# A linear-attention scan feeding a soft mixture of experts: forward scans moved to the head of a slot, the chunk states copied, and the output mixed between the down products

## The chip, the cores and the metric

One core of a Trainium2 chip runs the whole kernel in one launch. Its engines are called as the profile calls them: PE (TensorE, with PEld for its weight loads), DVE (VectorE), ACT (ScalarE), POOL (GpSimd) and SP (SyncE, which here only issues DMAs). The metric is the device time of one execution in microseconds (us), the median of several runs. All data is fp32.

## The reference, cut to what matters

```python
B, H, S, D = 4, 8, 768, 48                  # r, k, v, w: B x H x S x D;  u: H x D
for t in range(S):                          # linear attention with a decaying state
    cur = outer(u * k[t], v[t])
    y[t] = r[t] @ (state + cur)             # state: B x H x 48 x 48
    state = w[t][:, None] * state + outer(k[t], v[t])
x = y as (3072 tokens, 384)
logits = x @ phi                            # 32 slots = 8 experts x 4
d = softmax of logits over the tokens;  slot_input = d.T @ x
for e in range(8):                          # F = 1024
    slot_out[e] = relu(slot_input[e] @ w1[e]) @ w2[e]
out = softmax of logits over the slots @ slot_out
```

## The kernel before, in words

**Chunks.** The 768 steps of a head are cut into 6 chunks of 128. Inside a chunk the recurrence becomes matrix products: with G the product of decays from a step to the end of its chunk and its reciprocal counterpart from the start, keys are multiplied by G and queries by the forward products. Scores of a chunk are keys against queries, masked to earlier steps, and what comes from earlier chunks goes through a state of 48 x 48 at each chunk border. The term with u (the bonus) is a number a for each step and head, multiplied into v; the product is the tile `av`.

**Slots.** Two heads are worked on together, so there are 16 slots j = 4b + g (batch b, pair of heads g). The 128 partitions hold heads 2g and 2g+1 at partitions 0 to 47 and 64 to 111, and the 16 partitions left over by each carry a third of heads 6 and 7. So three units n0 = 3b, n0+1, n0+2 carry a batch, and in the fourth slot (g = 3) the keys and queries are put together in `g4` by six small DMAs from SBUF to SBUF (`gather`, two for each unit).

A slot does, on PE: `e_kn` (transpose the scaled keys, L565), `e_scores` (L575, 24 matmul records), `e_u` (L611, what each chunk adds to the state), `e_av` (L633, masked scores of the slot before against v), `e_a` (L591, the bonus numbers), `e_inter` (L640 adds `av` of the even head with an identity as weights, L647 adds queries times state). On DVE: three masked evictions of scores (L584), `state` (L620, a scan along the chunks that writes `Se`), `f_scan` (L525, L526, forward products of one unit), `g_scan` (L518, backward products), half of `c_y` (L657, y plus `av` into x). On POOL: a mask on a fourth of the scores (L581, after an ACT copy, L580), `p_k` (L535) and `p_r` (L539), which multiply keys and queries in place by the products, `p_rk` (L531), `p_av` (L606). On ACT: evictions. The scan `Se` is kept as [48, 6], chunk innermost, and is the moving operand of L647 with a step of 6 numbers; there is one `Se`.

In three of four slots a unit is prepared for the next slot (`state_n`: `f_scan`, then `p_r`) and another for the slot after it (`state_g`: `g_scan`, then `p_k`). Three of four slots also hold a piece of the expert part for the batch before: `x_turn` (L92, L660), `l_mm` (L97), `s_max`, `s_exp`, `s_mm` (L136), `s_norm`. A dummy matmul (`fill`, L489) stands at the end of each slot.

**What sets the order.** The schedule is written out by hand: each engine runs its instructions in the order of the program text, in one queue, and semaphores make it wait for its operands. The loop is in L730 to L808. In it `state(j)` stands after `e_inter(j - 1)`, `f_scan` after `state`, `p_r` after `f_scan`. All DMAs go through SP's queue in program order: keys and queries (`ld_kr`), decays (`ld_w`), values (`ld_v`), gathers, and the expert weights in pieces of 512 KB (`ld_w1`, `ld_w2`). PSUM has four rotating banks (`rot`) and four fixed ones (`cst`, `up`, `y0`, `y1`). SBUF is cut into 16 bins; expert weights are loaded into bins whose first contents are no longer needed.

**After the loop** (L813 to L901): the last slot's y, the logits of the last batch, the slot softmax brought together (`m_spread`, `m_factor`, `m_den`, `m_slots`), `up_proj` (L218), `turn`, then for a column group of 256 and one of 128 (`COLS`): `down_proj` (L251), `so_rep` (L258 to L261), `mix` (L276 to L283: products into four banks, evictions by DVE and ACT, a DMA to the output). `range_check` between the groups sets a flag; if a product of decays left its range, a slower form of the whole is run.

Of the kernel before, what the change touches and what calls it, by code (L numbers as in the profile page):

```python
# [18 lines left out]
P = 128  # L19
# [24 lines left out]
N_FILL0 = 14  # L44
N_FILL = (1,) * NIT
N_CHAIN = 2
W1_BINS = (9, 10, 11, 12, 13, 14, 15, 3)
W2_BINS = (4, 5, 6, 7, 8, 0, 2, 1)
PIECES = (0, 1, 1, 1, 1, 1, 1, 2, 1, 2, 1, 2, 2, 2, 1, 1)
SHARED = (0, 1, 1, 1) + (1,) * 12  # L50
PE_HEADS = (0,)
COLS = ((0, 256), (256, 384))
# [3 lines left out]
def rwkv_soft_moe(ctx: ExitStack, tc: tile.TileContext, wl, krl, vl, um, phil, w1l, w2l, r, k, v, w, u, out):  # L56
# [12 lines left out]
    nc.vector.tensor_reduce(out=r32.rearrange("p o s -> p (o s)"),  # L69
                            in_=ident.rearrange("p (g s) -> p s g", s=NS), axis=AX.X, op=ALU.add)  # L70
    rmat = const.tile([P, 4, NS], F32, name="rmat")
    nc.vector.tensor_copy(out=rmat, in_=r32.broadcast_to([P, 4, NS]))
    other = const.tile([TG, NTG, NS], F32, name="other")
    nc.vector.tensor_scalar(other, r32[0:TG].broadcast_to([TG, NTG, NS]), -BIG, BIG, op0=ALU.mult, op1=ALU.add)
# [4 lines left out]
    asum = const.tile([P, 2, C], F32, name="asum")  # L79
    cn = const.tile([P, NT, NS], F32, name="cn")  # L80
# [102 lines left out]
    def m_factor(b, q, bc):  # L183
        new = nM[:, b % 2:b % 2 + 1]
        bm = small.tile([TG, NTG, NS], F32, name="bm", bufs=1)
        nc.vector.tensor_tensor(out=bm, in0=bc, in1=other, op=ALU.add)
        mt = small.tile([TG, 1], F32, name="mt")
        nc.vector.tensor_reduce(out=mt, in_=bm, axis=AX.XY, op=ALU.min)
        fr = small.tile([TG, 1], F32, name="fr")
        nc.scalar.activation(out=fr, in_=new, func=AF.Exp, bias=mt, scale=-1.0)  # L190
        q["rf"] = rf = small.tile([TG, NS], F32, name="rf")
        nc.vector.tensor_scalar(rf, r32[0:TG, 0], fr, None, op0=ALU.mult)

    def m_den(q, bank):
        dp = bank([P, 1, NS], "den")
        nc.tensor.matmul(out=dp[:, 0, :], lhsT=ssum.broadcast_to([TG, P]), rhs=q["rf"], start=True, stop=True)
        q["den"] = den = small.tile([P, 1, NS], F32, name="den")
        nc.vector.tensor_scalar(den, dp, 1e-9, None, op0=ALU.add)
        nc.vector.reciprocal(out=den, in_=den)

    def m_slots(q, siT, bank):
# [3 lines left out]
        for st_ in range(2):  # L205
# [3 lines left out]
            nc.vector.tensor_tensor(  # L209
                out=dst, in0=sT.rearrange("p k (g a j) -> p k g a j", g=4, a=2)[:, :, :, st_],  # L210
                in1=q["den"].broadcast_to([P, KT, NS]).rearrange("p k (g a j) -> p k g a j", g=4, a=2)[:, :, :, st_],
                op=ALU.mult)
# [32 lines left out]
    def down_proj(hT, so, w2t, cg):  # L245
        lo, hi = COLS[cg]
        for st_ in range(2):
            for ft in range(FT):
                for g in range(4):
                    e = 4 * st_ + g  # L250
                    nc.tensor.matmul(  # L251
                        out=so[32 * g:32 * g + NS, :], lhsT=hT[ft // 2].rearrange(
                            "p (f e s) -> p f e s", f=2, e=E)[:, ft % 2, e, :],
                        rhs=w2t[e][:, FT * lo + ft * (hi - lo):FT * lo + (ft + 1) * (hi - lo)],
                        start=(st_ == 0 and ft == 0), stop=(st_ == 1 and ft == FT - 1))

    def so_rep(so, so_sb, rep, bank):
        nc.vector.tensor_copy(out=so_sb, in_=so)  # L258
        rp = bank(list(so_sb.shape), "rp")
# [11 lines left out]
    def mix(cT, rep, o, row, bank, parts=((0, 4), (4, 6))):  # L271
        ov = o.rearrange("p (n q t) -> p q n t", q=4, t=P)
        for lo, hi in parts:
            ops = [bank([P, hi - lo, P], "op") for _ in range(4)]
            for q in range(4):
                nc.tensor.matmul(out=ops[q].rearrange("p n t -> p (n t)"), lhsT=rep[32 * q:32 * q + NS, :],  # L276
                                 rhs=cT[32 * q:32 * q + NS, lo * P:hi * P], start=True, stop=True)
            for q in range(4):
                if q % 2:
                    nc.scalar.copy(out=ov[:, q, lo:hi, :], in_=ops[q])  # L280
                else:
                    nc.vector.tensor_copy(out=ov[:, q, lo:hi, :], in_=ops[q])
            nc.sync.dma_start(out=out[row:row + P, 512 * lo:512 * hi], in_=o[:, 512 * lo:512 * hi])  # L283
# [3 lines left out]
    def recompute():  # L287
# [114 lines left out]
        with tc.tile_pool(name="f_w", bufs=E) as f_w, tc.tile_pool(name="f_t", bufs=1) as f_t, \  # L402
# [32 lines left out]
            for cg, (lo, hi) in enumerate(COLS):  # L435
                so = f_pa.tile([P, hi - lo], F32, name="so")
                down_proj(hT, so, ws[1], cg)
                so_rep(so, so_sb[:, lo:hi], rep[:, lo:hi], bank)
                for row in range(lo, hi, P):
                    mix(cT, rep[:, row:row + P], o, row, bank)  # L440
# [25 lines left out]
    pat = cut(2, X + C * D, C * D)  # L466
    kr_b = [cut(3 + n, 0, KRW) for n in range(4)]
    w_b = [cut(3 + n, KRW, WC) for n in range(2)]
    G_b = [cut(6 + n, KRW, WC) for n in range(2)]
    v_b = [cut(n, KRW + lo, 2 * C * D) for n, lo in ((3, WC), (4, WC), (5, 576), (6, WC))]  # L470
    av = cut(5, KRW, 2 * C * D).rearrange("p (h c e) -> p h c e", h=2, e=D)
    g4 = cut(7, 0, KRW)
    kn = cut(7, KRW + WC, (C - 1) * PITCH).rearrange("p (c e) -> p c e", e=PITCH)
    at_b = [[[cut(8, 384 * (4 * n + 2 * h + hf), 384).rearrange("p (c t) -> p c t", t=P) for hf in range(2)]
             for h in range(2)] for n in range(2)]
    raw = cut(14, 0, 2 * S)
# [16 lines left out]
    def ld_w(n, lo=0, hi=C):  # L493
        a, z = CP * lo, CP * hi + 1
        nc.sync.dma_start(out=w_b[n % 2][:, a:z], in_=wl[n][:, a:z])

    def ld_kr(n, lo=0, hi=C):
        nc.sync.dma_start(out=kr_b[n % 4][:, 0:2 * S].rearrange("p (a t) -> p a t", a=2)[:, :, lo * P:hi * P],
                          in_=krl[n][:, :, lo * P:hi * P])

# [14 lines left out]
    def g_scan(n, lo=0, hi=C):  # L515
        G, wt = G_b[n % 2], w_b[n % 2]
        a, z = CP * lo, CP * hi + 1
# [11 lines left out]
    def p_rk(n, src=None):  # L529
        kr = kr_b[n % 4] if src is None else src  # L530
        nc.gpsimd.tensor_tensor(out=rk_b[n % 2], in0=kr[:, 0:S], in1=kr[:, S:2 * S], op=ALU.mult)  # L531

    def p_k(n, lo=0, hi=C):
        kv = kr_b[n % 4][:, lo * P:hi * P].rearrange("p (c t) -> p c t", t=P)
        nc.gpsimd.tensor_tensor(out=kv, in0=kv, in1=chunks(G_b[n % 2], 2, lo, hi), op=ALU.mult)  # L535

    def p_r(n, lo=0, hi=C):
        rv = kr_b[n % 4][:, S + lo * P:S + hi * P].rearrange("p (c t) -> p c t", t=P)
        nc.gpsimd.tensor_tensor(out=rv, in0=rv, in1=chunks(w_b[n % 2], 0, lo, hi), op=ALU.mult)  # L539
# [160 lines left out]
    nc.vector.tensor_copy(out=later.rearrange("p o t -> p (o t)"), in_=mk)  # L700
    for n in range(2):
        nc.gpsimd.memset(cut(8, 1536 * n, 1536), 0.0)
    for n in range(4):
        nc.gpsimd.memset(kr_b[n][:, 2 * S:2 * S + 1], 0.0)
    fill(N_FILL0)
    for hf in range(2):
        cs = (HC * hf, HC * hf + HC)
        g_scan(0, *cs)
        f_scan(0, *cs)
        kv = kr_b[0][:, 0:2 * S].rearrange("p (a t) -> p a t", a=2)[:, :, cs[0] * P:cs[1] * P]  # L710
        nc.scalar.copy(out=raw.rearrange("p (a t) -> p a t", a=2)[:, :, cs[0] * P:cs[1] * P], in_=kv)
        p_k(0, *cs)
        p_r(0, *cs)
        e_scores(0, hf)
    c_ends(0)
    c_chk(0)
    nc.sync.dma_start(out=phi_sb, in_=phil)
    ld_kr(2)
    ld_v(2)
    ld_kr(3)  # L720
    ld_w(2)
    p_rk(1)
    g_scan(1)
    p_k(1)
    c_ends(1)
    p_rk(0, raw)
    nc.gpsimd.memset(g4, 0.0)

    qs = {}
    for j in range(NIT):  # L730
        b, g = divmod(j, NG)
        pb = b - 1
        n0 = 3 * b
        if g == 1:
            gather(n0)
        if g == 2:
            gather(n0 + 1)
            gather(n0 + 2)
        e_kn(j)
# [5 lines left out]
        state_n = {0: n0 + 1, 1: n0 + 2, 3: n0 + 3}.get(g)  # L745
        state_n = state_n if state_n is not None and state_n < NU else None
        state_g = {0: n0 + 2, 2: n0 + 3, 3: n0 + 4}.get(g)
        state_g = state_g if state_g is not None and state_g < NU else None
        if j:
            e_av(j - 1)  # L750
        if unit(j) is not None:
            e_a(unit(j))
        if j:
            e_inter(j - 1)
        state(j)
        if state_n is not None:
            f_scan(state_n)
            p_r(state_n)
            c_chk(state_n)
        if j:  # L760
            c_y(j - 1)
        if g == 0 and n0 + 2 < NU:
            p_rk(n0 + 2)
        if g == 2 and n0 + 3 < NU:
# [193 lines left out]
```

## Time and profile before

| | us |
|---|---|
| median of 3 runs | 286.93 |
| lowest, highest | 285.36, 287.54 |
| the profiled execution | 285.88 |
| its span | 284.2 |
| PE busy | 216.8 |
| DVE busy | 117.3 |
| POOL busy | 96.9 |
| ACT busy | 60.3 |
| mean granted PE clock | 0.785 of 2.4 GHz |

The span runs from the first to the last instruction of the profiled execution. Busy time is the time in which an engine had an instruction under way, and a busy PE is not a PE at full speed: its clock is granted at one of two levels, and a mean between 0.5 and 1 says how the stretch was shared by the two. Slot 0's first transposes start at 17.8 us, slot 1's at 26.0, and the loop ends at 221.7.

### The profile page before, as it was taken

The numbers are of one execution on the slowest core, as the hardware profiler recorded it, in microseconds if no ns is written. First come the engines' busy times: TensorE is split into PE (matmuls) and PEld (weight loads), VectorE is DVE, ScalarE is ACT, GpSimd is POOL, SyncE is SP. The second block draws the span as 40 slices with busy tenths as digits, with TensorE's granted clock in tenths as the row PEclk, the third lists the DMA queues.
The fourth block names the chain that finished last, engine by engine and source line by source line (L and its number), as shares of the span: only waits on it lengthen the run. The fifth ranks groups of instructions, "written<-read, shape, count | busy, mean of one in ns | idle before, by whom it ended". The sixth has DMA issues, their size and how long they took to land.

```text
span 284.2 us, 7354 instructions
## 1 busy us (share of the span) xinstructions
PE 216.8 (76%) x3190; PEld 162.0 (57%) x3190; DVE 117.3 (41%) x203; ACT 60.3 (21%) x185; POOL 96.9 (34%) x95
## 2 busy tenths in 40 slices
PE   7247949749496978749899869496999978997740
PEld 2136848639394855639488738393888633353510
DVE  5556252562624265662432466625223432114430
ACT  2112111212122330321230313212221220112220
POOL 5259533436363341844231436453011200200000
PEclk9655777795969989995555597869557999999985
DMA  5960455635063863615382507921971499960933
GB/s 158 362 223 8 122 181 159 228 111 175 2 200 114 226 232 110 230 40 181 111 259 67 205 2 253 327 63 16 340 269 15 133 417 405 410 254 39 405 121 114
DMA packets 15174, 51.77 MB, mean 182 GB/s; under 512 B 2208, under 2 KB 2976, under 8 KB 14752
## 3 DMA queue, kind: packets, MB, share of 16 engines
q1 hardware_dynamic: 15136, 51.23, 52.4%
q8 instruction: 27, 0.44, 0.7%
q14 instruction: 11, 0.09, 0.1%
HBM read 44.14 MB, written 4.72 MB: 172 GB/s over the span
## 4 chain that ended last, share of the span: by engine, by line
PE 63%; DVE 22%; ACT 4%; issue 3%; POOL 2%; DVEq 0%; ACTq 0%; POOLq 0%
PE sc L575 15%; PE y L633 11%; DVE bin L526 7%; PE y L647 6%; DVE bin L518 6%; PE up L611 5%; PE y L640 4%; PE hp L218 4%; PE so L251 4%; PE ap L591 4%; DVE bin L620 3%; PE op L276 3%; ACT bin L660 2%; PE kp L565 1%; PE lp L97 1%
## 5 line engine op out<-in xcount | busy, mean ns | idle before, releaser
L575 PE MATMUL sc<-bin 48*128 48x128 f32 x384 | 45.3, 389 | 33.5 <-ACT bin L660 16.3
L575 PEld LDWEIGHTS sc<-bin 48*128 48x128 f32 x384 | 40.0, 282 | 38.0 <-POOL bin L539 30.4
L620 DVE TENSOR_TENSOR_SCAN bin<-up,bin 112x288 f32<-112x288 f32 x16 | 12.1, 756 | 77.7 <-PE y L647 75.9
L584 DVE COPY_PREDICATED bin<-later,sc 128x384 f32<-128x384 int32 x49 | 26.4, 581 | 34.1 <-PE sc L575 34.0
L633 PE MATMUL y<-bin,bin 128*64 128x48 f32 x768 | 35.3, 267 | 0.0
L633 PEld LDWEIGHTS y<-bin,bin 128*64 128x64 f32 x768 | 34.2, 187 | 0.3 <-issue 0.3
L535 POOL TENSOR_TENSOR bin<-bin,bin 128x768 f32<-128x768 f32 (+1 forms) x13 | 20.5, 1577 | 11.5 <-DVE bin L518 7.7
L539 POOL TENSOR_TENSOR bin<-bin,bin 128x768 f32<-128x768 f32 x6 | 10.1, 1676 | 36.8 <-DVE bin L526 36.8
L518 DVE TENSOR_TENSOR_SCAN bin<-bin,cst 128x775 f32<-128x775 f32 (+1 forms) x13 | 21.2, 1631 | 2.2 <-DMA bin<-in_wl_dram 2.2
L531 POOL TENSOR_TENSOR bin<-bin 128x768 f32<-128x768 f32 x12 | 21.7, 1807 | 0.0
L526 DVE TENSOR_TENSOR_SCAN bin<-bin,cst 128x774 f32<-128x774 f32 (+1 forms) x13 | 21.4, 1642 | 0.4
L606 POOL TENSOR_TENSOR bin<-bin,asb 128x576 f32<-128x576 f32 x12 | 14.0, 1164 | 20.6 <-DVE bin L657 20.6
L539 POOL TENSOR_TENSOR bin<-bin 128x768 f32<-128x768 f32 (+1 forms) x7 | 10.2, 1464 | 29.2 <-DVE bin L526 29.2
L647 PEld LDWEIGHTS y<-bin,bin 48*64 48x64 f32 x640 | 15.2, 161 | 7.3 <-issue 7.3
L647 PE MATMUL y<-bin,bin 48*64 48x48 f32 x640 | 18.2, 273 | 0.0
L565 PE MATMUL kp<-ident,bin 112*128 112x112 f32 x80 | 13.4, 304 | 5.9 <-ACT bin L660 2.4
L611 PE MATMUL up<-bin,bin 128*48 128x48 f32 x320 | 15.9, 274 | 2.2 <-ACT bin L567 2.2
L611 PEld LDWEIGHTS up<-bin,bin 128*48 128x48 f32 x320 | 13.4, 182 | 5.7 <-ACT bin L567 2.6
L489 PE MATMUL zero<-zb 128*128 128x512 bf16 x40 | 15.2, 463 | 1.3 <-DVE cst L693 1.3
L565 PEld LDWEIGHTS kp<-ident,bin 112*128 112x128 f32 x80 | 10.8, 167 | 9.2 <-issue 3.5
L581 POOL TENSOR_SCALAR_AFFINE_SELECT bin<-bin 128x384 f32<-128x384 f32 x15 | 7.8, 522 | 23.9 <-ACT bin L580 23.9
L580 ACT COPY bin<-sc 128x384 f32<-128x384 f32 x15 | 7.2, 479 | 31.9 <-PE sc L575 31.9
(114 smaller groups left out, 261.5 us busy)
## 6 DMA issues: line engine op xcount, KB each, us to landing
bin<-in_w1l_dram SPq DMA_DIRECT2D x24, 512.0 KB, 5.9
bin<-in_w2l_dram SPq DMA_DIRECT2D x24, 512.0 KB, 9.9
bin<-in_krl_dram SPq DMA_DIRECT2D x11, 768.0 KB, 4.4
bin<-in_vl_dram SPq DMA_DIRECT2D x16, 288.0 KB, 3.9
bin<-in_wl_dram SPq DMA_DIRECT2D x11, 387.5 KB, 3.1
out_dram<-bin SPq DMA_DIRECT2D x3, 1024.0 KB, 4.7
bin<-bin SPq DMA_DIRECT2D x24, 96.4 KB, 6.1
out_dram<-bin SPq DMA_DIRECT2D x3, 512.0 KB, 5.0
```

Of the source, the lines that this page charges most:

```text
L518: nc.vector.tensor_tensor_scan(out=G[:, a:z][:, ::-1], data0=wt[:, a:z][:, ::-1], data1=cst[:, 0:1].broadcast_to([P, z - a]), initial=1.0, ...
L526: nc.vector.tensor_tensor_scan(out=wt[:, a:z], data0=wt[:, a:z], data1=cst[:, 1:2].broadcast_to([P, z - a]), initial=1.0, op0=ALU.mult, op ...
L531: nc.gpsimd.tensor_tensor(out=rk_b[n % 2], in0=kr[:, 0:S], in1=kr[:, S:2 * S], op=ALU.mult)
L535: nc.gpsimd.tensor_tensor(out=kv, in0=kv, in1=chunks(G_b[n % 2], 2, lo, hi), op=ALU.mult)
L539: nc.gpsimd.tensor_tensor(out=rv, in0=rv, in1=chunks(w_b[n % 2], 0, lo, hi), op=ALU.mult)
L565: nc.tensor.transpose(out=kp[:, c - lo, :], in_=kr[0:PITCH, P * c:P * c + P], identity=ident[0:PITCH, 0:PITCH])
L575: nc.tensor.matmul(out=sc[h][:, c, :], lhsT=kr[head(h), lo:lo + P], rhs=kr[head(h), S + lo:S + lo + P], start=True, stop=True)
L584: nc.vector.copy_predicated(out=at, mask=later.broadcast_to([P, HC, P]), data=sc[h])
L611: nc.tensor.matmul(out=up[head(h), :, n + 1], lhsT=kn[:, n, head(h)], rhs=vt(j)[:, h, n, :], start=(n == 0), stop=(n == C - 2))
L620: nc.vector.tensor_tensor_scan(out=Se[0:PITCH], data0=up[0:PITCH].rearrange("p e n -> p (e n)"), data1=pat[0:PITCH], initial=0.0, op0=ALU. ...
L633: nc.tensor.matmul(out=yb[h][rows, c, :], lhsT=at[:, rows], rhs=vt(j)[:, h, c, :], start=(c == 0), stop=False)
L647: nc.tensor.matmul(out=yb[h][rows, c, :], lhsT=kr[head(h), lo:lo + HALF], rhs=Sv[head(h), c, :], start=False, stop=(c == C - 1))
```

## The change

Eight things, in the order of the program.

1. Start: the first three units are loaded raw into `raw_b` (two of the loads on ACT's DMA queue), so that `p_k` and `p_r` write from there into `kr_b` and the ACT copy of the raw data goes. All scans of units 0 and 1 come first, then their products, then the scores of slot 0. Constants for the rows (`row_constants`) are made in slot 3, some clearing moves from POOL to ACT, and there are more dummy matmuls (26, and 4 after each half of the first scores).
2. `f_scan(ahead)` is the first thing that DVE does in a slot, and `state(j)` comes right after `e_u(j)`.
3. `state` is followed by an ACT copy of `Se` into `Sc[j % 2]`, chunk outermost; `e_inter` reads `Sc`.
4. The identity matmul of L640 goes. `c_y` evicts the even head with ACT and adds `av` to it with POOL. `p_av` stands at the head of the next slot. After the last slot DVE does both heads, in halves (`c_y_last`).
5. `e_inter(j - 1)` and `c_y(j - 1)` stand at the end of a slot, behind the expert part's products and `g_scan`/`p_k`.
6. DMAs move inside a slot, one gather stands a slot earlier, pieces of the weights are spread otherwise over the slots, and the bins of the weights change.
7. The slots' sums are not divided by the softmax denominator before `up_proj`; `so_scale` divides the expert output instead, a number for each partition.
8. `COLS` is three groups of 128, and `mix` of a group runs between the parts of the next group's `down_proj`.

```diff
-N_FILL0 = 14
+N_FILL0 = 26
+N_START = (4, 4, 4)
-PIECES = (0, 1, 1, 1, 1, 1, 1, 2, 1, 2, 1, 2, 2, 2, 1, 1)
+PIECES = (0, 0, 1, 1, 2, 1, 1, 2, 2, 2, 2, 2, 2, 2, 1, 0)
-PE_HEADS = (0,)
-COLS = ((0, 256), (256, 384))
+COLS = ((0, 128), (128, 256), (256, 384))
...
+    def so_scale(so, so_sb):
+        nc.vector.tensor_scalar(so_sb, so, den, None, op0=ALU.mult)
...
     def state(j):
...
+        nc.scalar.copy(out=Sc[j % 2][0:PITCH].rearrange("p (n e) -> p n e", e=D),
+                       in_=Se[0:PITCH].rearrange("p (e n) -> p n e", n=C))
...
-        Sv = Se.rearrange("p (e n) -> p n e", n=C)
-        for h in PE_HEADS:
-            nc.tensor.matmul(out=yb[h].rearrange("p c e -> p (c e)"), lhsT=ident,
-                             rhs=av[:, h].rearrange("p c e -> p (c e)"), start=False, stop=False)
+        Sv = Sc[j % 2].rearrange("p (n e) -> p n e", e=D)
...
     def c_y(j):
+        dst = y_of(j, 0)
+        nc.scalar.copy(out=dst, in_=ys[j][0])
+        nc.vector.tensor_tensor(out=y_of(j, 1), in0=ys[j][1], in1=av[:, 1], op=ALU.add)
+        nc.gpsimd.tensor_tensor(out=dst, in0=dst, in1=av[:, 0], op=ALU.add)
...
     fill(N_FILL0)
...
+    for hf in range(2):
+        g_scan(0, HC * hf, HC * hf + HC)
+        f_scan(0, HC * hf, HC * hf + HC)
+    g_scan(1)
+    f_scan(1)
+    for hf in range(2):
+        p_k(0, HC * hf, HC * hf + HC)
+        p_r(0, HC * hf, HC * hf + HC)
+    c_ends(0)
+    c_chk(0)
+    p_k(1)
+    p_r(1)
+    c_ends(1)
+    c_chk(1)
+    for hf in range(2):
+        e_scores(0, hf)
+        fill(N_START[hf])
...
     for j in range(NIT):
+        ahead = {0: n0 + 1, 1: n0 + 2, 3: n0 + 3}.get(g)
...
+        later_g = {0: n0 + 2, 2: n0 + 3, 3: n0 + 4}.get(g)
...
+        if j > 2:
+            p_av(j - 1)
         if g == 1:
             gather(n0)
+            gather(n0 + 1)
         if g == 2:
-            gather(n0 + 1)
             gather(n0 + 2)
+        if ahead is not None:
+            f_scan(ahead)
         e_kn(j)
         if j:
             e_scores(j, 0)
             e_scores(j, 1, ((1, 1), (0, 1))[0:SHARED[j]])
         c_pat(j)
         e_u(j)
+        state(j)
         if j:
             e_av(j - 1)
-        if unit(j) is not None:
-            e_a(unit(j))
-        if j:
-            e_inter(j - 1)
-        state(j)
-        if state_n is not None:
-            f_scan(state_n)
-            p_r(state_n)
-            c_chk(state_n)
-        if j:
-            c_y(j - 1)
...
+        if ahead is not None:
+            p_r(ahead)
+            c_chk(ahead)
...
+        if later_g is not None:
+            g_scan(later_g)
+            if later_g > 2:
+                p_rk(later_g)
+            p_k(later_g)
+        if j:
+            e_inter(j - 1)
+            c_y(j - 1)
...
+    down_proj(hT, sos[0], w2t, 0)
+    scale(0)
+    for cg in range(1, 3):
+        down_proj(hT, sos[cg], w2t, cg, 0, 5)
+        spread(cg - 1)
+        down_proj(hT, sos[cg], w2t, cg, 5, 10)
+        mix_part(cg - 1, 0, any_bank)
+        if cg == 1:
+            range_check()
+        down_proj(hT, sos[cg], w2t, cg, 10, 15)
+        mix_part(cg - 1, 1, any_bank)
+        down_proj(hT, sos[cg], w2t, cg, 15, 16)
+        scale(cg)
+    spread(2)
+    mix_part(2, 0, any_bank)
+    mix_part(2, 1, last_bank)
```

Where the loop's lines are left out, there stand, behind `c_chk(ahead)` and in this order: `ld_w`, `ld_v`, the slot's pieces of weights, `x_turn`, `s_dturn` with `s_rows`, `e_a`, `l_mm` with `s_max`, `s_mm` with `s_acc` and `s_sum`; and behind `c_y(j - 1)`: `s_exp` with `s_keep`, `c_ends(later_g)`, `fill`, `ld_kr`.

## Rows read from the trace of the kernel before

**Rows 1.** Busy time by stretch: start:end, length; PE, PEld, DVE, ACT, POOL; PEclk; DMA; GB/s.

```profile
26.00:63.70 37.70, 28.72 (x480) 24.87 (x478) 15.87 (x22) 6.54 (x23) 16.65 (x14) 0.77 0.48 152
63.70:221.70 158.00, 130.24 (x2047) 106.86 (x2047) 68.94 (x108) 37.39 (x122) 62.74 (x57) 0.75 0.49 157
115.20:127.30 12.10, 8.00 (x172) 6.93 (x173) 7.70 (x13) 3.31 (x12) 7.39 (x8) 1.00 0.44 147
127.30:143.00 15.70, 14.86 (x184) 11.07 (x185) 4.89 (x8) 3.10 (x10) 6.73 (x6) 0.52 0.47 141
143.00:158.00 15.00, 13.84 (x174) 11.92 (x172) 5.08 (x10) 3.35 (x12) 3.85 (x5) 0.50 0.64 192
236.50:250.00 13.50, 13.16 (x112) 4.47 (x112) 3.14 (x13) 2.14 (x7) 1.80 (x1) 1.00 1.02 406
250.00:284.20 34.20, 19.86 (x311) 11.17 (x310) 8.87 (x23) 5.83 (x14) 0.00 (x0) 0.86 0.45 178
```

**Rows 2.** Waits of the whole span: engine, line, releaser; us in total, times, longest.

```profile
DVE bin L620 <- PE y L647: 75.9, 15, 7.2
POOL bin L539 <- DVE bin L526: 65.9, 12, 9.0
```

**Rows 3.** Chain that ended last, from slot 1 to slot 2: start, length, what.

```profile
34.51 1.10 PE y L647 x39
...
36.58 1.78 DVE bin L526
38.43 1.69 POOL bin L539
40.16 2.93 PE sc L575 x24
```

**Rows 4.** The same chain in slot 8, PE's clock at its upper level.

```profile
117.96 1.40 PE y L633 x48
...
120.03 0.68 PE y L640 x2
120.71 1.10 PE y L647 x40
```

**Rows 5.** The same chain in slot 10, PE's clock at its lower level.

```profile
148.37 2.56 PE y L633 x48
...
153.40 1.32 PE y L647 x40
```

**Rows 6.** Groups of instructions of the whole span: busy us, mean ns; idle before.

```profile
L584 DVE COPY_PREDICATED bin<-later,sc 128x384 f32<-128x384 int32 x49 | 26.4, 581 | 34.1 <-PE sc L575 34.0
...
L526 DVE TENSOR_TENSOR_SCAN bin<-bin,cst 128x774 f32<-128x774 f32 (+1 forms) x13 | 21.4, 1642 | 0.4
...
L606 POOL TENSOR_TENSOR bin<-bin,asb 128x576 f32<-128x576 f32 x12 | 14.0, 1164 | 20.6 <-DVE bin L657 20.6
...
L539 POOL TENSOR_TENSOR bin<-bin,bin 128x768 f32<-128x768 f32 x6 | 10.1, 1676 | 36.8 <-DVE bin L526 36.8
...
L617 ACT COPY bin<-bin 112x288 f32<-112x288 f32 x16 | 7.0, 435 | 0.0
```

**Rows 7.** DMA issues of the gathers: KB each, median us to landing.

```profile
bin<-bin SPq DMA_DIRECT2D x24, 96.4 KB, 6.1
```

**Rows 8.** Timeline of DVE's first scan: start, length, engine, line.

```profile
7.07 0.96 DVE L518 TENSOR_TENSOR_SCAN bin<-bin,cst 128x388 f32<-128x388 f32 x1 [2.23 <-DMA bin<-in_wl_dram]
```

**Rows 9.** Chain that ended last, behind the loop: down products and last eviction.

```profile
250.09 7.09 PE so L251 x128
...
266.83 3.61 PE so L251 x126
...
271.78 1.15 PE op L276 x8
...
275.02 0.41 DVE bin L282
```

More of the change, by code (lines that the diff above doesn't have):

```diff
@@ L437, in recompute @@
                 down_proj(hT, so, ws[1], cg)
[L438 to L440 removed]
+                so_scale(so, so_sb[:, lo:hi])
+                so_rep(so_sb[:, lo:hi], rep[:, lo:hi], bank([P, P], "rp"))
+                for n0, n1 in ((0, 4), (4, 6)):
+                    mix(cT, rep[:, lo:hi], o, lo, lambda q, shape, name: bank(shape, name), n0, n1)
     manual = ExitStack()
@@ L744, in rwkv_soft_moe @@
         e_u(j)
[L745 to L748, printed above, removed]
+        state(j)
         if j:
             e_av(j - 1)
-        if unit(j) is not None:
-            e_a(unit(j))
-        if j:
-            e_inter(j - 1)
-        state(j)
-        if state_n is not None:
-            f_scan(state_n)
-            p_r(state_n)
-            c_chk(state_n)
-        if j:
-            c_y(j - 1)
-        if g == 0 and n0 + 2 < NU:
-            p_rk(n0 + 2)
-        if g == 2 and n0 + 3 < NU:
-            p_rk(n0 + 3)
-        if g == 3 and n0 + 4 < NU:
-            p_rk(n0 + 4)
-        p_av(j)
-        if state_g is not None:
-            g_scan(state_g)
-            p_k(state_g)
-            c_ends(state_g)
+        if ahead is not None:
+            p_r(ahead)
+            c_chk(ahead)
+        nw = {0: n0 + 3, 1: n0 + 4, 3: n0 + 5}.get(g)
+        if nw is not None and 4 <= nw < NU:
+            ld_w(nw)
+        if j + 3 < NIT and j > 2:
+            ld_v(j + 3)
+        weights(PIECES[j])
+        if g == 0 and pb >= 0:
+            x_turn(pb, 1)
         if g == 1 and pb >= 0:
             x_turn(pb, 2)
+        if g == 3:
+            x_turn(b, 0)
+        if g == 2 and pb >= 0:
+            s_dturn(qs[pb], rot)
+            s_rows(qs[pb], rot)
+            s_rows_exp(qs[pb])
+        if 1 <= j <= 2:
+            e_a(j - 1)
+            p_av(j - 1)
+        if j > 1 and unit(j) is not None:
+            e_a(unit(j))
+        if g == 1 and pb >= 0:
             lp = rot([TG, 2, P], "lp")
@@ L789, in rwkv_soft_moe @@
             s_sum(pb, qs[pb])
-            s_norm(pb, qs[pb])
-        if g == 3:
-            x_turn(b, 0)
-        if g == 0 and pb >= 0:
-            x_turn(pb, 1)
+        if later_g is not None:
[3 more added lines that the diff above has]
+            p_k(later_g)
+        if g == 2 and pb >= 0:
+            s_norm(pb, qs[pb])
+        if j:
+            e_inter(j - 1)
+            c_y(j - 1)
+        if g == 1 and pb >= 0:
+            s_exp(pb, qs[pb])
+            s_keep(qs[pb])
+        if later_g is not None:
+            c_ends(later_g)
+        if j == 1:
+            p_rk(1)
+            p_rk(2)
+        if j == 3:
+            row_constants()
+        if j < 3:
+            ld_v(j + 3)
         fill(N_FILL[j])
@@ L799, in rwkv_soft_moe @@
             ld_kr(m + 4)
-        nw = {0: n0 + 3, 1: n0 + 4, 3: n0 + 5}.get(g)
-        if nw is not None and 3 <= nw < NU:
-            ld_w(nw)
-        if j + 3 < NIT:
-            ld_v(j + 3)
-        weights(PIECES[j])
+        if j == 13:
+            for i in range(KT):
+                ld_w1(E - 1, i)
         if j == 14:
             for i in range(KT):
-                ld_w1(E - 1, i)
+                ld_w2(0, i)
     weights(99)
     lb = B - 1
+    p_av(NIT - 1)
     siT = rk_b[1].rearrange("p (a s) -> p a s", s=NS)
     nc.gpsimd.memset(siT, 0.0)
+    for e in (1, 2):
+        for i in range(KT):
+            ld_w2(e, i)
     e_av(NIT - 1)
-    e_inter(NIT - 1)
+    for i in range(KT):
+        ld_w2(3, i)
     x_turn(lb, 1)
     lp = own([TG, 2, P], "lp", "cst")
+    e_inter(NIT - 1)
     for kt in range(2):
         l_mm(kt, xT[:, kt], lp)
-    c_y(NIT - 1)
+    c_y_last(NIT - 1)
     for i in range(2):
-        for e in range(E - 2):
+        for e in (4, 5):
             ld_w2(e, i)
@@ L852, in rwkv_soft_moe @@
     fill(N_CHAIN)
+    m_den(q, rot)
     hps = [own([P, 512], f"hp{n}", f"y{n}") for n in range(2)]
```

209 lines of the change are left out of this document (103 added, 106 removed).

## The prediction

> **What bounds the kernel now.** I read the stretches first: 158.0 of the 284.2 us span are slots 4 to 15, in which PE is busy for 130.2 us, DVE for 68.9, POOL for 62.7 and ACT for 37.4 [rows 1]. So PE is the bound there, but in two ways at once: it stands idle for 28 us, and its clock is granted at a mean of 0.75. As the clock has two levels, half of the time is spent at 1.2 GHz.
>
> The waits say where the idle time starts. DVE's state scan waits 75.9 us in 15 slots for the last matmuls of `e_inter`, and POOL's `p_r` waits 65.9 us for the forward scan behind it [rows 2]. The chain shows it in order: `e_inter` (34.51), state scan, forward scan (36.58), `p_r` (38.43), and only at 40.16 the scores of the next slot [rows 3]. From the end of `e_inter` (35.6) to the scores are 4.6 us in which PE has only a dummy matmul and the five transposes. The reader is to see that the scan waits for nothing that it computes with: there is one `Se`, which `e_inter` of the slot before still reads, and the forward scan merely stands behind it in DVE's queue.
>
> Then the clock. Slot 8 has 8.00 us of PE work at clock 1.00; slots 9 and 10 have 14.86 and 13.84 us at 0.52 and 0.50, and there PE is busy for 95% and 92% of the time [rows 1]. Slot 8's stretch ends in four idle microseconds, after which the clock is at its lower level. So a pause costs twice: itself, and slots at half clock behind it.
>
> **The sum, part by part** (against the span of 284.2 us; the profiled execution took 285.88, 1.7 more, and the median of the runs is 1.05 above that).
>
> *PE's work in a slot.* At the upper level 48 records of `e_av` take 1.40 us and 40 of `e_inter` 1.10 [rows 4], at the lower 2.56 and 1.32 [rows 5]: 2.50 against 3.88, a ratio of 0.64; as `e_inter` scales least I take 0.62. Slot 9's 14.86 then is 9.2, slot 10's 13.84 is 8.6; slot 8 has 8.00 and some 0.4 of transposes ahead of its stretch. Less the identity matmuls, 0.68 at the upper level [rows 4], these are 8.5, 7.9 and 7.7: 8.0 on average. The fourth kind (no `e_a`, but `s_mm`) I set equal.
>
> *The other engines.* A twelfth of the long stretch is 5.7 us of DVE, 5.2 of POOL, 3.1 of ACT [rows 1]. New is an ACT copy of 288 numbers (0.435 for such a copy [rows 6], so 3.6) and a POOL addition of 288: half of `p_av`'s 576 in 1.164 [rows 6], so an estimate of 0.6 and 5.8 in all; its bounds are 0.4 and 1.2, and 6.4 still fits. All stay under 8.0.
>
> *The chain through the slot.* DVE's `c_y` still waits for `e_inter`, and the forward scan comes right behind it, so it starts as late as before; but its unit is needed one slot later than DVE's place in the queue now suggests. Counted from the last `e_inter`: some 0.5 for `c_y`, 1.8 for the scan with its reciprocal, and `p_r` behind `p_av` and the mask, which wait for the scores (about 3.5), so about 5.5 with its 1.7 [rows 6]. The next scores come at about 8.9. That is 3.4 us of slack in place of a wait of 4.6. What is late next: the three score evictions (0.58 each [rows 6]) stand behind the scan, and the fourth pair of PSUM banks in rotation is wanted by `x_turn` at some 4.8 us; they are done at 4.0 to 4.4. And `c_ends` stands in ACT's queue in front of the next slot's transposed keys and waits for `g_scan`, last on DVE in a slot with `s_mm`: about 0.8, twice in four slots. With the gathers I take 0.5 of waits a slot, with bounds of 0 and 2.0. So 8.5 us for 12 slots: 102 us. Without idle stretches the clock should stay up as it does in slot 8; I add 5 us for one drop (a slot at half clock costs 14.35 - 1.3 = 13.0, so 4.5 more). 107 instead of 158.
>
> *The first slots.* DVE's first scan starts at 7.07 when its data is there [rows 8]. Four half scans of 0.96 with small work between end at 11.4, the two of unit 1 (1.64 [rows 6] each) at 15, the first scores' evictions at 17.3, slot 0's keys and sums about 4 later, as before: slot 1 at 21.5 instead of 26.0. Bounds: 19 to 26. Slots 1 to 3 take 37.7 now [rows 1]; I take 8.5 each and 2.0 for three products of POOL (`p_rk`) that pile up there: 27.5. Slot 4 starts at 49.0. The raw loads, the clearing on ACT, and the row constants in slot 3 I cost at nothing: ACT has half of its slot free, DVE 2 us; uncovered they would be 3 us once.
>
> *Queues that steps are moved past.* On SP `ld_w` still waits for `p_r`, some 6 us into a slot, with `ld_v` and weights queued behind it; all are wanted a slot or more later. Only the last gather of a batch is wanted within a slot: 6.1 us to landing [rows 7] against 8.0. The loop's transfers stay the same: 157 GB/s at a share of 0.49 [rows 1] become 232 and 0.72 in 107 us. They fit. Behind the loop 406 GB/s at a share of 1.02 [rows 1] say that `w2` comes as fast as it can; fewer pieces are left then (one expert goes into the loop), and a third of the columns is enough to start, so I cost it at nothing; each piece that is late is 1.3 us.
>
> *Behind the loop* 62.5 us remain (284.2 - 221.7). The identity matmuls of the last slot (0.68 [rows 4]) and the two DVE instructions of the denominator leave the path: 1.5, bounds 0 and 2. The down products are 7.09 and 3.61, with the mix of the first group between, and the last eviction ends at 275.4 [rows 9]. Afterwards PE has three products of 3.6, three `rp` of 0.5, two mixes of 1.8, the range check, for which it still waits 2.6 (two evictions and five small instructions of DVE), and handoffs of 1.0: 19.5 from 250.1, where it is 21.7 now until the last mix (271.78 [rows 9]). Minus 2.3; bounds 0 and 5. Taken together 58.5.
>
> *Contiguous states.* I cost them at 0 on PE: 40 records in 1.10 us are 27.5 ns each against 29.2 for the contiguous `e_av` [rows 4]. The Trainium skill (SBUF — State Buffer, in "Door 1: The DMA port swizzle") says that reads that step past 16 bytes pay for each new line, which would make these matmuls faster after the copy. The Trainium skill (TensorE: Matmul & The Clock Gate, "Back-to-back issue gap") puts a floor of 25 ns on the start-to-start time, whatever the operand; the trace's 27.5 ns agrees with that one, and by both the sum would fall by no more than 1.6 us (2.5 ns, 40 records, 16 slots).
>
> Sum: 21.5 + 27.5 + 107 + 58.5 = 214.5 us of span, 216.2 with the 1.7 around it; the median of such runs may be 1 us higher.
>
> **Rivals.**
>
> *A, the clock is lost in half of the slots.* For: slots 9 and 10 show PE busy for over 90% and still at half clock, so that being busy alone did not bring it back [rows 1]. Against: in slot 8 it held through 8 us of the same work. 7.5 slots of 14.0 (slots 9 and 10 without the identity matmuls, their remaining waits kept) and 7.5 of 8.5 are 169 + 21.5 + 58.5, with the 1.7: 250 us.
>
> *B, transfers become late.* A share of 0.72 leaves less room, and the last gather has two microseconds to spare. If a whole landing of 6.1 us [rows 7] shows in each batch, 24 us: 240. At 3 us each: 228.
>
> *C, the wait only moves.* `c_y`, forward scan and evictions stand in one queue behind `e_inter`. If the banks or the state come 4 us late in each slot, as `p_r` does now, slots stay at 12.6 to 13.2 and only the ends gain: 286 - 4.5 - 4.0, about 278 to 284. Against: it needs DVE to be four microseconds behind PE's order, where I find 0.4 to spare and some 2 us late in one slot of four.
>
> *D, slower.* If the new order puts pauses in the middle of slots (evictions behind the scan) and PE never gets its upper clock in the loop, all 15 slots cost what slots 9 and 10 do, 15.35 less 1.3: 14.0 each, 211, with 21.5, 58.5 and 1.7: 292. It decides from a mean of 13.6 us a slot on, with a granted clock of little over 0.5 throughout, where the loop now has 0.75.
>
> **Chances.** My forecast with its own spread (203 to 227): 0.64. A and cases between: 0.14. B: 0.12. C: 0.06. D: 0.04. A measurement of this kernel tells about 1% from no change. C's slow end is no change: 0.04; D slower: 0.04; the rest faster: 0.92. The range goes from 202 (no waits, no clock lost, the tail's bounds) to 242, with B and the better part of A.
>
> **What would show it.** Right: the state scan no longer waits for `e_inter`; slots of 8 to 9 us; a clock of 0.95 or more in slots 4 to 15; PE over 90% busy there; first scores of slot 1 near 22 us. Wrong: scores that still wait for `p_r`, or `x_turn` for DVE's evictions; stretches of 0.5 in the clock while PE is busy (A, D); transposes of a fourth slot that wait for a gather (B). A mean slot above 10 us makes the prediction wrong.

## The result, and the profile after

| | before | after |
|---|---|---|
| median, us | 286.14 (4 runs) | 212.9 (4 runs) |
| ratio, with its 95% interval | | 0.7417 (0.7326 to 0.7508) |
| span of the profiled execution, us | 284.2 | 210.2 |
| mean granted PE clock | 0.785 | 0.914 |

Forecast were 216.2 us, between 202 and 242. Here and below a median is over all runs of a kernel, and a ratio compares the fast runs alone (those within 1.5% of the fastest of their kernel). The stretches after, in the columns of [rows 1], are the start up to slot 1, slots 1 to 3, slots 4 to 15, and the part from the down products on:

```profile
0.00:16.20 16.20, 13.95 (x83) 6.80 (x85) 10.55 (x18) 6.18 (x11) 10.62 (x21) 1.00 0.76 257
16.20:43.50 27.30, 23.13 (x493) 21.00 (x492) 17.22 (x22) 10.09 (x28) 20.64 (x17) 0.81 0.67 208
43.50:152.30 108.80, 97.47 (x2033) 81.29 (x2031) 71.91 (x116) 45.37 (x133) 68.85 (x67) 0.91 0.77 249
...
178.70:210.20 31.50, 18.36 (x441) 13.24 (x440) 8.77 (x25) 5.34 (x14) 0.00 (x0) 0.91 0.42 166
```

The reader is to see where the 74 us of span went. A slot starts here with its transposes. [rows 1] cuts the kernel before at 63.7, just ahead of the scores of slot 4 (64.35), but slot 4's transposes start there at 59.6. Cut at the transposes, as after, the two stretches before are:

```profile
26.00:59.60 33.60, 28.04 (x475) 24.44 (x474) 11.91 (x18) 5.96 (x20) 14.61 (x12) 0.75 0.46 148
59.60:221.70 162.10, 130.92 (x2053) 107.29 (x2051) 72.89 (x113) 37.97 (x124) 64.78 (x58) 0.76 0.49 158
```

So the start is 9.8 us shorter (26.0 to 16.2), slots 1 to 3 6.3 us (33.6 to 27.3), slots 4 to 15 53.3 us (162.1 to 108.8), all behind the loop 4.6 us (62.5 to 57.9). In slots 4 to 15 PE is now busy for 90% of the time, at a clock of 0.91 where it had 0.76.

The two waits of [rows 2] are gone. What the state scan still waits for is its own input, 3.9 us in all:

```profile
DVE bin L633 <- PE up L625: 3.9, 5, 1.7
```

The chain of two neighbouring slots, 7 and 8 (start, length, what), answers to [rows 3] and [rows 4]:

```profile
64.38 5.61 DMA bin<-in_w1l_dram
69.99 1.16 PE kp L579 x5
71.16 2.86 PE sc L589 x24
...
78.71 0.73 PE y L659 x40
79.44 0.32 PE zero L497
79.76 0.48 PE kp L579 x5
80.24 0.92 PE sc L589 x12
...
83.44 1.40 PE y L648 x48
```

At 78.71 to 80.24 one slot runs into the next without a pause, where [rows 3] had 4.6 us. But slot 7, a fourth slot, starts late: PE has finished slot 6 at 66.3 and stands until a DMA lands at 70.0, and its scores then take 2.86 us, the lower clock. The profile puts the wait down to the weights' DMA that came last; the transposes read `g4`, which the gather fills (gather_early, below, tells the two apart). All fourth slots (3, 7, 11, 15) show such a pause, 0.8 to 3.7 us. The page's DMA rows (KB each, median us to landing) have the gathers slower than in [rows 7]:

```profile
bin<-bin SPq DMA_DIRECT2D x24, 96.4 KB, 7.5
```

### The profile page after: what moved, and what is told of

It reads as the page before. It is cut to its first block, busy times and chain, and to the rows that moved or that the text cites. A ratio compares the mean times of both kernels' runs of the same rounds, so it can differ in the third digit from the quotient of the medians.

```text
span 210.2 us, 7632 instructions
## 1 busy us (share of the span) xinstructions
PE 177.1 (84%) x3306; PEld 133.2 (63%) x3308; DVE 115.7 (55%) x207; ACT 72.2 (34%) x202; POOL 104.5 (50%) x108
## 4 chain that ended last, share of the span: by engine, by line
PE 54%; DMA 24%; DVE 8%; POOL 5%; issue 2%; SPq 1%; ACT 1%; ACTq 0%; DVEq 0%; POOLq 0%
DMA bin<-bin 14%; PE sc L589 10%; PE y L648 8%; DMA bin<-in_w1l_dram 6%; PE so L257 5%; PE hp L224 5%; DMA bin<-in_krl_dram 4%; PE xp L96 4%; PE up L625 3%; PE kp L579 3%; PE y L659 3%; PE sp L140 3%; PE op L282 2%; POOL bin L553 2%; PE ap L605 2%
## 5 line engine op out<-in xcount | busy, mean ns | idle before, releaser
L589 PE MATMUL sc<-bin 48*128 48x128 f32 x384 | 34.3, 315 | 5.0 <-ACT bin L581 2.8
L589 PEld LDWEIGHTS sc<-bin 48*128 48x128 f32 x384 | 29.4, 215 | 9.7 <-ACT bin L581 4.9
L549 POOL TENSOR_TENSOR bin<-bin,bin 128x768 f32<-128x768 f32 (+1 forms) x13 | 20.3, 1563 | 18.7 <-issue 11.6
L648 PEld LDWEIGHTS y<-bin,bin 128*64 128x64 f32 x768 | 27.7, 155 | 1.2 <-ACT bin L668 0.5
L530 DVE TENSOR_TENSOR_SCAN bin<-bin,cst 128x775 f32<-128x775 f32 (+2 forms) x13 | 21.2, 1628 | 2.4 <-DMA bin<-in_wl_dram 2.4
L670 POOL TENSOR_TENSOR bin<-bin,bin 128x288 f32<-128x288 f32 x15 | 10.6, 705 | 12.7 <-ACT bin L668 8.0
L581 ACT COPY bin<-kp 128x336 f32<-128x336 f32 (+1 forms) x32 | 11.1, 397 | 13.4 <-PE kp L579 13.4
L553 POOL TENSOR_TENSOR bin<-bin,bin 128x768 f32<-128x768 f32 (+1 forms) x9 | 13.7, 1518 | 0.0
L257 PE MATMUL so<-bin,bin 128*32 128x128 f32 x384 | 12.2, 274 | 0.0
L497 PEld LDWEIGHTS <-zb 128*128 128x128 bf16 x60 | 6.0, 110 | 9.2 <-issue 5.0
L257 PEld LDWEIGHTS so<-bin,bin 128*32 128x32 f32 x384 | 10.2, 110 | 2.0 <-issue 1.7
```

Source lines behind the costliest of these rows:

```text
L257: nc.tensor.matmul(out=so[32 * g:32 * g + NS, :], lhsT=hT[ft // 2].rearrange("p (f e s) -> p f e s", f=2, e=E)[:, ft % 2, e, :], rhs=w2t[e ...
L497: nc.tensor.matmul(out=z, lhsT=zb[:, 0:P], rhs=zb, start=True, stop=True)
L530: nc.vector.tensor_tensor_scan(out=G[:, a:z][:, ::-1], data0=wt[:, a:z][:, ::-1], data1=cst[:, 0:1].broadcast_to([P, z - a]), initial=1.0, ...
L549: nc.gpsimd.tensor_tensor(out=io[0], in0=io[1], in1=chunks(G_b[n % 2], 2, lo, hi), op=ALU.mult)
L553: nc.gpsimd.tensor_tensor(out=io[0], in0=io[1], in1=chunks(w_b[n % 2], 0, lo, hi), op=ALU.mult)
L589: nc.tensor.matmul(out=sc[h][:, c, :], lhsT=kr[head(h), lo:lo + P], rhs=kr[head(h), S + lo:S + lo + P], start=True, stop=True)
```

## The experiments

Each kernel is the changed one with one edit, unless it says that it starts from the kernel before. All ratios are to the kernel before, run beside it. The changed kernel itself, once more:

> The changed kernel once more, unaltered, as the yardstick for the kernels run with it: 210 to 215 us.

Measured: 213.1 us (median of 6, from 206.5 to 216.8). That agrees with 212.9. The spread is wide: a difference of two or three microseconds between two of the kernels below tells nothing.

### Which move shortened the loop

Forward scan back behind `e_inter`:

```diff
-        if ahead is not None:
-            f_scan(ahead)
         e_kn(j)
...
-        if ahead is not None:
-            p_r(ahead)
-            c_chk(ahead)
...
             e_inter(j - 1)
+        if ahead is not None:
+            f_scan(ahead)
+            p_r(ahead)
+            c_chk(ahead)
```

The decays' load (`ld_w`) moves with them, behind `c_y`.

> The changed kernel with the forward scan, p_r and the decays' load moved back behind e_inter, the state scan left early. If the scan's place is the cause: p_r ends 1 to 3 us behind the time at which the next scores could start, in three of four slots, and the clock falls after some of these pauses: 228 to 258 us. If it was the single state buffer: within 4 us of the changed kernel, 211 to 217 us.

Measured: 246.9 us, ratio 0.8601 (0.8498 to 0.8705): 34 us slower than the changed kernel. The scores wait for `p_r` again, in 11 slots (first line, a wait: us in total, times, longest), and the chain shows the sequence of [rows 3] again, scan, `p_r`, scores at the lower clock:

```profile
PEld sc L589 <- POOL bin L553: 35.8, 11, 4.8
```

```profile
71.34 1.78 DVE bin L538
73.19 1.69 POOL bin L553
74.93 2.93 PE sc L589 x24
```

State scan and its copy back behind `e_inter`:

```diff
-        state(j)
         if j:
             e_av(j - 1)
...
             e_inter(j - 1)
+        state(j)
+        if j:
             c_y(j - 1)
```

> The changed kernel with the state scan and its ACT copy moved back behind the matmuls of e_inter; the forward scan stays first in a slot. If the forward scan's place is what removed the wait before the scores, next to nothing is lost: 212 to 218 us, and no scores wait for p_r. If the state's wait for e_inter was the cause, the idle time in front of the scores comes back: 235 us or more.

Measured: 226.7 us, 14 slower, between the two expectations and by a way that neither named. No scores wait for `p_r`; they wait for ACT:

```profile
ACT Sc L636 <- DVE bin L633: 17.8, 6, 4.0
...
PEld sc L589 <- ACT bin L581: 15.0, 7, 3.8
```

The copy of the state stands in ACT's queue and waits for the late scan; behind it stand the evictions of the next slot's transposed keys (L581), which hold the PSUM banks that the second half of the scores needs. So the early state is worth 14 us of its own, and these waits put it down to its ACT copy; no run has the late scan without the copy.

Both back:

> The changed kernel with both the state scan and the forward scan, p_r and the decays' load moved back behind e_inter: the order of the loop before, with everything else of the change kept. If the order is what shortened the loop, the old pause in front of the scores is back in three of four slots and only the start, the tail, the identity matmuls and the contiguous reads are left as gains: 255 to 272 us. If the two moves overlap, the late state adds nothing to the late forward scan: 244 to 250 us.

Its edit is the two above together.

Measured: 264.1 us, ratio 0.916 (0.9081 to 0.924), 51 us slower than the changed kernel; 34 and 14 add up to 48, so the two moves hardly overlap. The wait for `p_r` is back at 37.7 us. The first expectation holds. The place of the two scans is thus worth some 51 us in the changed loop. The profiled execution of this kernel is 20 us shorter than that of the kernel before: 9.8 us in the start, 3.6 in slots 1 to 3, 5.3 in slots 4 to 15 (156.7 against 162.1) and 1.3 behind the loop.

Yet this is not quite the order of the loop before. There the forward scan and `p_r` stood ahead of `g_scan` and `p_k`, and behind the start `p_r` waited 4.5 to 9.0 us for the scan in each of its slots. In late_fscan and late_both `g_scan` and `p_k` stand ahead of them, since point 5 of the change is kept, and behind the start `p_r` follows `p_k` on POOL without a wait for the scan in three of nine slots. How the 74 us are shared between the scans' place, point 5 and points 6 and 7 no run tells exactly.

### What is left in the loop

The last gather of a batch a slot earlier:

```diff
-        if g == 2:
-            gather(n0 + 2)
...
             p_r(ahead)
+            if g == 1:
+                gather(n0 + 2)
             c_chk(ahead)
```

> The changed kernel with the last gather of a batch issued a slot earlier, right behind its p_r. If the pauses of 0.8 to 3.7 us in front of the transposes of every fourth slot are waits for that gather, they go, and with them the lower clock behind them: 198 to 206 us. If the gather only waits for the other transfers and comes no earlier, or another wait stands behind it: 209 to 213 us.

Measured: 201.8 us, 11 less than the changed kernel. The transposes no longer wait for any DMA, and the clock is higher. This kernel's slots 1 to 3 and 4 to 15 (columns as above):

```profile
16.10:38.40 22.30, 20.28 (x494) 18.46 (x493) 17.11 (x23) 9.99 (x28) 19.29 (x17) 0.92 0.77 250
38.40:139.40 101.00, 91.64 (x2033) 76.25 (x2031) 71.11 (x116) 45.11 (x133) 70.38 (x67) 0.98 0.80 263
```

In the changed kernel the same slots take 12.8 us more (27.3 and 108.8). Its four pauses add up to 9.2 us of idle PE, but PE's idle time in these slots falls by only 4.1 us (15.5 to 11.4), since other waits grow. Its busy time falls by 8.7 (120.6 to 111.9): most of the gain is the same work done at the higher clock. This version is faster than both kernels. Two further kernels that contain it, below, have ratios of 0.6998 and 0.6978, with intervals clear of the changed kernel's; the 14 runs of the three took 198.0 to 207.2 us, the ten of the changed kernel 206.5 to 216.8.

The pauses are not the same in each execution. In the profile of changed_again the transposes waited 2.2, 0.6 and 0.6 us for gathers, and in slot 15 for none. Slots 4 to 15 still took 108.2 us at a clock of 0.91, and in slot 10 PE stood for 2.3 us between two matmuls of `e_inter`, for which the profile names no releaser.

The pauses filled with dummy matmuls:

```diff
-N_FILL = (1,) * NIT
+N_FILL = (1, 1, 8, 1) * (NIT // 4)
```

> The changed kernel with 8 dummy matmuls instead of 1 at the end of the third slot of each batch, just ahead of the transposes that wait for the last gather. If a pause costs twice (itself, and a lower clock behind it), the pause filled with work keeps the clock at its upper level in the fourth slots and 3 to 8 us are gained in all: 205 to 210 us. If the clock falls for another reason, or the fill only adds to the wait: 212 to 220 us.

Measured: 211.2 us, ratio 0.7378 (0.731 to 0.7446), not to be told from 0.7417. In slot 3 the mechanism is seen. Its transposes start at the same time in both kernels (34.9), since the gather comes no earlier. With the fill the scores take 1.57 us and slot 4's transposes start at 41.0:

```profile
34.93 0.67 PE kp L579 x5
35.60 1.57 PE sc L589 x24
...
41.02 0.48 PE kp L579 x5
```

Without it, in the changed kernel, they take 2.86 and slot 4 begins 2.5 us later, at 43.5:

```profile
34.94 1.16 PE kp L579 x5
36.10 2.86 PE sc L589 x24
38.97 0.97 PE up L625 x20
```

In slot 7 the wait outlasted the fill by 1.5 us, and the clock fell all the same. So in slot 3 the pause cost the clock behind it as well; in sum no gain is shown. In this execution PE also stood for 3.9 us in slot 9 (94.17 to 98.08), again without a releaser that the profile names.

The lock on a small DVE instruction, on top of the early gather:

```diff
-        nc.vector.tensor_scalar(rm, rm, 1e-9, None, op0=ALU.add)
+        nc.scalar.activation(out=rm, in_=rm, func=AF.Copy, bias=1e-9)
```

> The last gather a slot earlier, and the addition of 1e-9 in s_norm moved from DVE to ACT. In the changed kernel that DVE instruction on 128 x 6 numbers took 1.55 us and ended with a POOL instruction, with the forward scan queued behind it. If it was held by POOL, three batches gain 1.4 us each on DVE and 2 to 4 us of the time: 197 to 200 us. If DVE has that time to spare: 200 to 203 us, as with the early gather alone.

Measured: 201.5 us, ratio 0.6978 (0.6915 to 0.7041): no gain over 201.8 that could be told, with single runs from 198.4 to 207.2. The instruction itself (ns, least, median, most) went from this, in the kernel with the early gather,

```profile
L173 DVE TENSOR_SCALAR rm<-rm x4: 171/868/1583, 63.2 to 157.5; 128x6 f32<-128x6 f32 x4
```

to this:

```profile
L173 ACT ACTIVATE rm<-rm x4: 207/208/208, 66.3 to 158.3; 128x6 f32<-128x6 f32 x4
```

So the instruction is cheap on ACT, but the 2 to 4 us did not come. That DVE had the time to spare is not shown: in the kernel with the early gather, the chain that ended last passes through this instruction twice (63.16 and 99.64).

### Contiguous states and the bonus

Two state buffers without the copy:

```diff
-            out=Se[0:PITCH], data0=up[0:PITCH].rearrange("p e n -> p (e n)"), data1=pat[0:PITCH],
+            out=Sc[j % 2][0:PITCH], data0=up[0:PITCH].rearrange("p e n -> p (e n)"), data1=pat[0:PITCH],
...
-        nc.scalar.copy(out=Sc[j % 2] ...)
...
-        Sv = Sc[j % 2].rearrange("p (n e) -> p n e", e=D)
+        Sv = Sc[j % 2].rearrange("p (e n) -> p n e", n=C)
```

> The changed kernel without the ACT copy of the state: the state scan writes two buffers in turn, chunk innermost, and e_inter reads them with a step of 6 numbers. If contiguous states make e_inter faster (0.73 us against 1.10 before), it is back at 1.1 us and the kernel loses 4 to 7 us: 217 to 220 us. If the step costs nothing and the 0.37 us came from something else: 212 us or a little less, as ACT has 0.7 us a slot less to do.

Measured: 210.7 us, ratio 0.7303 (0.7237 to 0.7368), against 0.7417 (0.7326 to 0.7508): no loss. On PE the step does cost: `e_inter` takes 1.03 us in its chain at the upper clock, 0.73 in the changed kernel.

```profile
83.70 1.03 PE y L657 x40
```

The ACT copy that buys these 0.3 us takes 0.72 us a slot, more than the 0.435 of [rows 6] for the same 288 numbers written from a broadcast. That the two cancel is a guess; in the time neither can be told. With the early gather, where PE waits less, it is the same:

> The last gather a slot earlier and no ACT copy of the state (strided reads). With the gather's pauses gone PE should be nearer to the bound: if e_inter's 0.3 us a slot now count, 3 to 5 us slower than with the early gather alone, 205 to 207 us. If ACT's copy of 0.72 us costs as much as it gives: 199 to 203 us.

Its edit is that of the early gather and that of the strided reads together.

Measured: 201.2 us, ratio 0.6998 (0.6933 to 0.7062), against 201.8. So the change did not need the layout. That it needed the second buffer follows from the program and not from a run: with one buffer the early scan would overwrite what `e_inter` of the slot before has yet to read.

The identity matmul in place of POOL's addition:

```diff
         Sv = Sc[j % 2].rearrange("p (n e) -> p n e", e=D)
+        if j < NIT - 1:
+            nc.tensor.matmul(out=yb[0].rearrange("p c e -> p (c e)"), lhsT=ident,
+                             rhs=av[:, 0].rearrange("p c e -> p (c e)"), start=False, stop=False)
...
-        nc.gpsimd.tensor_tensor(out=dst, in0=dst, in1=av[:, 0], op=ALU.add)
```

> The changed kernel with the even head's av added by an identity matmul on PE again (15 slots), and without POOL's addition. If PE is the bound of a slot, its 0.65 us a slot come back, and with waits in four slots that swallow some of it: 3 to 9 us more, 216 to 222 us. If POOL's queue was what held slots up, freeing 0.7 us of it a slot pays for the matmul: 209 to 214 us.

Measured: 215.6 us (211.7 to 218.4), 2.6 above the changed kernel's medians, whose own runs spread from 206.5 to 216.8. That falls in the gap between the expectations, and no interval tells them apart: it stays open what moving half of the bonus to POOL brought. Its profiled execution speaks for both sides: slots 4 to 15 took 105.5 us, less than the 108.8 of the changed kernel, though PE was busy for 102.3 of them, as no transposes waited for a gather; slots 1 to 3 took 33.3 us at a clock of 0.69.

### Start and tail

From the kernel before, the second half of the first decays one column later:

```diff
     def ld_w(n, lo=0, hi=C):
-        a, z = CP * lo, CP * hi + 1
+        a, z = CP * lo + (lo > 0), CP * hi + 1
...
     def g_scan(n, lo=0, hi=C):
-        a, z = CP * lo, CP * hi + 1
+        a, z = CP * lo + (lo > 0), CP * hi + 1
```

> The kernel before with one edit: the second half of the first decays is loaded and scanned from one column later, so that the two halves share no column. If the first scan waited for the second transfer only because of that column, it starts at 4.9 us (when DVE's copies of constants end) and not at 7.1, the first scores of slot 1 come 2 us earlier, and the time falls by 1 to 2 us. If it waited for its own data: no change in the scan's start.

Measured: ratio 0.9862 (0.979 to 0.9934), but this rests on the two fastest of eleven runs. The median of all eleven is 288.6 us, above the 286.1 of the kernel before, so a gain in time is not shown. The trace shows what the edit does. The first scan starts at 4.76, right behind DVE's constants, where [rows 8] had it at 7.07, and slot 1's transposes start at 23.4 where they started at 26.0:

```profile
4.61 0.23 DVE L74 TENSOR_SCALAR other<-r 96x96 f32<-96x96 f32 x1
4.76 0.94 DVE L518 TENSOR_TENSOR_SCAN bin<-bin,cst 128x388 f32<-128x388 f32 x1
```

So the first scan had been held by the second transfer, through one shared column. In the changed kernel, with the constants gone too, it starts at 3.44:

```profile
3.44 0.96 DVE L530 TENSOR_TENSOR_SCAN bin<-bin,cst 128x388 f32<-128x388 f32 x1 [1.73 <-DMA bin<-in_wl_dram]
```

Down products and mixes one after the other, still in three groups:

```diff
-        down_proj(hT, sos[cg], w2t, cg, 0, 5)
         spread(cg - 1)
-        down_proj(hT, sos[cg], w2t, cg, 5, 10)
         mix_part(cg - 1, 0, any_bank)
+        mix_part(cg - 1, 1, any_bank)
         if cg == 1:
             range_check()
-        down_proj(hT, sos[cg], w2t, cg, 10, 15)
-        mix_part(cg - 1, 1, any_bank)
-        down_proj(hT, sos[cg], w2t, cg, 15, 16)
+        down_proj(hT, sos[cg], w2t, cg)
```

> The changed kernel with the three down products and the mixes one after the other, not interleaved (still three groups of 128). If interleaving brought the 2.3 us that the sum has for it: 214 to 217 us, and the part behind the products' first start is 2 to 4 us longer. If the order of the tail is worth nothing, since DVE and ACT evict for as long either way: 211 to 214 us.

Measured: 218.6 us, ratio 0.7538 (0.7478 to 0.7599), 0.012 above the changed kernel's, or 3.5 us; the two intervals overlap by a little. The traces say it more sharply. From the first down product to the last mix PE takes 25.1 us one after the other (177.83 to 202.94),

```profile
202.07 0.50 PE rp L267 x2
...
202.94 1.18 PE op L282 x8
```

and 20.0 interleaved, in the changed kernel (178.74 to 198.73):

```profile
178.74 5.01 PE so L257 x168
183.75 0.42 PE rp L267 x2
184.16 1.23 PE so L257 x40
185.39 1.11 PE op L282 x8
186.50 1.27 DVE bin L288 x2
...
188.78 0.16 PE fp L931
188.94 1.15 PE so L257 x39
...
198.73 1.18 PE op L282 x8
```

Three groups one after the other are slower than the two of before (21.7 us, [rows 9]). Each group has its own waits for evictions, and the second product took 5.8 us (187.55 to 193.40, a clock of 0.74) where the first took 3.7 at a clock of 1.00. It is the interleaving that pays for the third group. From 186.5 to 188.9 PE still stands, for the range check.

## Why the prediction was right

**What bounds the loop.** Right. The pause before the scores was an order of queues, not a need of data: with the two scans placed early it is gone, and put back late a pause as long returns (late_fscan, late_both). Of the two, the forward scan's place was the larger. I did not see that the state scan's place would act through ACT's queue; that it takes part at all I had from the one `Se` alone. Of the signs I named, the mean slot came out at 9.1 us and PE's busy share at 90%, but the clock at 0.91 and not 0.95, and the transposes of fourth slots did wait for gathers, which I had listed as a sign of B.

**Slots 4 to 15:** 107 us forecast, 108.8 measured. The three terms behind it were each off, and that they cancel to 1.8 us is luck. PE's work: 20.5 us passed at the lower clock (68.2 to 75.1, 99.0 to 102.4 and 105.8 to 116.0), PE was busy for 16.6 of them, and at the ratio of 0.62 these cost 6.3 too many; so of 97.5 busy us 91 are left at the upper clock, or 7.6 a slot in place of 8.0. `e_inter` at 0.73 for 1.10 us is most of that difference. Waits: 6 us forecast, 11.3 measured (108.8 less 97.47), 6.7 of them at the gathers of slots 7, 11 and 15. Clock: 5 forecast, 6.3.

**Contiguous states.** The step that was wrong: 0 on PE, and it is 0.3 to 0.37 us a slot. 0.73 us for 40 records are 18.3 ns each, less than the 25 ns that I took for a floor. The comparison with `e_av` misled me too: its matmuls have 128 rows and those of `e_inter` 48, so its 29.2 ns bounds nothing here. The Trainium skill (SBUF — State Buffer, "Door 1: The DMA port swizzle") had it right that reads which step past 16 bytes pay; the trace of strided agrees, with 1.03 us for 0.73. The Trainium skill (TensorE: Matmul & The Clock Gate, "Back-to-back issue gap") states a floor of about 25 ns that these matmuls go below. In the time no difference could be told (strided, gather_strided).

**The start:** 21.5 forecast, 16.2 measured. I took the first scan's 7.07 as the arrival of its own data [rows 8]. It was that of the second half, and the diff's `(lo > 0)` takes the tie away; I had costed that edit at nothing. The first scan is 3.6 us earlier for it and for the constants that went to slot 3; the column alone brought 2.3 of these (start_overlap). The scans then were not what ended last: the chain of the start goes through the second half of the first raw keys, for which POOL waited until 9.97, a load that I had costed at nothing. The first scores were evicted at 14.5 where I had 17.3, and from there to slot 1 it took 1.7 us where I had 4.2.

**Slots 1 to 3:** 27.5 and 27.3, though the 37.7 that I set it against reaches into slot 4. **The tail:** 58.5 and 57.9; between the first down product and the last mix it fell by 1.7 us, for 2.3 forecast.

**The rivals.** B, late transfers, was there in part: four pauses of 0.8 to 3.7 us with the clock behind them, some 11 us in all (gather_early), where the forecast had them as a part of its 6 us of waits. The gathers took 7.5 us to land, where it was 6.1, at a share of the DMA engines of 0.77 for 0.49; no run takes the two apart. A appeared only for single slots: the clock fell in the pauses of slots 3 and 7, and at 105.8, a microsecond ahead of that of slot 11; the pause of slot 15 left it up. Once (99.0 to 102.4) it fell behind 1.5 us in which slot 10's scores stood, and it came back within the slot. C and D did not occur.

**The total.** The span was 210.2 us for a sum of 214.5: the start came out 5.3 us shorter than forecast, and the loop only 1.8 longer because its errors cancelled.

**The small terms.** POOL's addition took 0.705 us, 0.6 estimated; the ACT copy 0.72, 0.435 estimated, in a queue that has room.

## What to carry to other kernels

When an engine's queue holds work that needs nothing from the current step behind work that does, move it ahead and give shared results a second buffer; the stall that it caused elsewhere, and here the lower clock behind the stall, go together. Then look at what the shorter period leaves no time for: here a small transfer that had hidden in a slot of 13 us showed in one of 8, and issuing it a slot earlier gave another 11 us, most of them through the clock. A wait put down to a transfer may be for the neighbour's bytes: look for a shared element between two parts of a split load before taking a start time as given.

## What was not expected of the hardware

A moving operand read with a step of 24 bytes made 40 matmul records of 48 columns take 1.03 us, and 0.73 when contiguous, both at the upper clock. A DVE instruction on 128 x 6 numbers took up to 1.58 us, where its least was 0.17, and in the changed kernel it ended with a POOL product that had started just before it:

```profile
67.00 1.67 POOL L549 TENSOR_TENSOR bin<-bin,bin 128x768 f32<-128x768 f32 x1 [2.28 <-issue]
67.15 1.55 DVE L173 TENSOR_SCALAR rm<-rm 128x6 f32<-128x6 f32 x1
```

The Trainium skill (SBUF — State Buffer, "Who interferes with whom") says that an instruction of this kind can need a pair of ports that DVE shares with POOL, and that the engine which issues first holds it for its whole instruction; these numbers agree.
